# Attention and two feed-forward layers: seventh products into an output bank, larger batches in the shared bank, more groups in the seven-product form

## The chip, the cores and the metric

The kernel runs on one core of a Trainium2 chip. The metric is the device time of one execution in microseconds, the median of three runs.

## What is computed

`x` is an attention output over 6016 tokens of 256 channels, where the scores are channels against channels (256 x 256). Two feed-forward layers follow, with 2048 hidden features each:

```python
def _moe_ref(x, w_in, w_out):        # layer one
    h = x @ w_in
    r = np.maximum(h, 0.0)
    g = r * r
    return (g @ w_out).astype(np.float32)

def _moe2_ref(x, w_in, w_out):       # layer two
    h = x @ w_in
    g = np.maximum(0.01 * h, h)
    return (g @ w_out).astype(np.float32)
```

All data are fp32.

## The kernel before

**Tiling.** The tokens are cut into six pairs of halves, 512 tokens a half in five pairs and 448 in the fifth (`WIDTH`). The hidden features are cut into eight groups of 256 (`NG`), two blocks of 128 each. The layers run pair by pair, and in a pair group by group: 12 sweeps of eight groups, 96 units `n`. Layer one's first pair has the attention folded into its weights and a form of its own; the other 88 units are built by `unit`.

**Number form.** [...] Each fp32 operand is split into a high part (a cast by ScalarE) and a low part (a subtraction by VectorE, line 120), and a product is three matmuls (`mm3`): low by high, high by high, high by low.

**First products.** For one group the products of input and `w_in` form a 2 x 2 block product (two token halves, two feature blocks, two channel blocks). It is computed in seven block products, F1 to F7, in place of eight, after Strassen and Winograd. Two banks hold them, `ha` and `hb` (in plain pairs alternately `hc` and `he`). ScalarE copies a bank out between them (`C11`, `u`, `w`; line 1378), VectorE adds (`c22`, `c12`: `c<-w` and `c<-u`, line 570), and TensorE goes on in the same bank when the copy or sum is there. F6 is the seventh in order. The next group's F2 goes into a bank that ScalarE's copy `C11` has filled, and that copy waits for the sum `c12` of the group before.

**Second products.** A group's activations `g` times `w_out` add up in the output banks `y`: (half, channel block) = (0,0), (0,1), (1,0), (1,1), over all eight groups of a pair. A *plain* group needs eight products. A *shared* group (`form_of` is "S", listed in `GROUPS`) needs seven, P1 to P7 (`shared_item`, with the tables `FROM` and `TO`), after the same identity. For it VectorE forms four differences of activations (`sub`, line 1473), and ScalarE and VectorE make high and low parts of five operands: G0 and G1 (1024 columns), B22, T3 and T2 (512 columns). P2, P3 and P4 go into the output banks (0,1), (1,1) and (0,0); P5 into a bank F of its own; P1, P6 and P7 into one bank A in turn.

**Shared sums.** What stands in A is taken out by `take_shared` after every batch of two groups (`BATCH`): into P1, then U (P6), then V (P7). The first batch is copied by ScalarE, later ones are added by VectorE. Five shared groups make batches of two, two and one. At a pair's end `combine` (in the last pair `combine_last`) joins P1, U, V, F and the output banks in six additions of VectorE; in layer two the result is transposed and stored. Pairs with shared groups are called mixed: before, layer one's last two and all of layer two.

**What sets the order.** The kernel first plans: `build` lists tasks with an engine, a cost, a due time, what they depend on and which buffers they need (`Buf`; `link` makes the k-th user of a buffer wait for the user that had it before). `simulate` runs a list schedule with these costs (`PIPE` gives latencies), and `PE.choose` takes first products in order and fills between them with the second products that are ready. Several turns are made (`TURNS`); the plan with the earliest end for TensorE is written out. From there the order on each engine is fixed, and each engine executes in its order. All loads and stores are issued by SyncE, in order. Weights of shared groups are loaded in three parts: `wo` (512 KB), `ws` for P5 (128 KB) and `ws` for P6 and P7 (256 KB).

Of the kernel before, what the change touches and what calls it, by code (L numbers as in the profile page):

```python
# [26 lines left out]
def raw(ap):  # L27
    return ap.bitcast(F32)
# [3 lines left out]
def attn_moe_moe2(  # L32
# [22 lines left out]
    GROUPS = {(1, 4): (0,1,3,4,6), (1, 5): (0,1,3,4,6), **{(2, p): (0,1,3,4,6) for p in range(5)}, (2, 5): (0,1,3,4)}  # L55
# [61 lines left out]
    order.__enter__()  # L117
# [217 lines left out]
    with (  # L335
# [3 lines left out]
    ):  # L339
        acc = att.tile([P, 2, G, C], F32, name="acc")  # L340
# [313 lines left out]
    def shared(n, product, bank_key, first):  # L654
# [92 lines left out]
    def take_out(key, d):  # L747
# [73 lines left out]

    def simulate(pe):
        for i, x in enumerate(tasks):
            x.then, x.then_order = [], []
            if late_start and x.engine in ("DVE", "ACT"):
                x.due = late_start[i]
# [13 lines left out]
        while n:  # L840
# [109 lines left out]
    BATCH = 2  # L950
    FROM = {"P1": "G0", "P2": "G0", "P3": "B22", "P4": "G1", "P5": "G1", "P6": "T2", "P7": "T3"}
    TO = {"P1": "A", "P6": "A", "P7": "A", "P5": "F", "P2": ("y", 0, 1), "P3": ("y", 1, 1), "P4": ("y", 0, 0)}

    def batch_of(n):
        L, p, g = units[n]
        i = sorted(GROUPS[L, p]).index(g)
        return i // BATCH, i % BATCH

    def seeded(n):

        L, p, g = units[n]
        return L == 2 and not (p and g < 2 and WIDTH[p] > WIDTH[p - 1])
# [9 lines left out]
    def build(base):  # L972
# [141 lines left out]
        done = {}  # L1114
# [18 lines left out]
        def finish_plain(L, p):  # L1133
# [4 lines left out]
            for half in range(2):  # L1138
# [10 lines left out]
                b = T("DVE", 3.1 * s, due + 0.1, take_out, key, 1, deps=done[L, p, half, 1] + [a], uses=[o])  # L1149
# [165 lines left out]

        def load_wo(n):
# [50 lines left out]

# [430 lines left out]
```

## Time and profile before

| | us |
|---|---|
| median of three runs | 1013.92 |
| lowest and highest | 1013.14, 1014.22 |
| the profiled execution | 1014.96 |
| its span, first to last instruction | 1013.2 |
| TensorE busy | 1005.3 |
| VectorE busy | 878.5 |
| ScalarE busy | 793.5 |

The profile is of one execution. "Busy" is the time in which at least one instruction of the engine ran; instructions of VectorE and ScalarE overlap a little at their ends, so the distance between the starts of two queued ones is shorter than the duration of either. The granted clock of TensorE is 0.999 of its 2.4 GHz level over the span.

### The profile page before, as it was taken

How to read it: one execution, taken by the hardware profiler on the slowest of the kernel's cores; microseconds unless marked ns; L12 is line 12 of the kernel's file. 1: busy time of each engine (PE TensorE's matmuls, PEld its weight loads, DVE VectorE, ACT ScalarE, POOL GpSimd, SP SyncE). 2: the span in 40 equal slices, each digit the busy share in tenths (PEclk: the TensorE clock that was granted, in tenths of full speed). 3: DMA queues.
4: the chain of work that ended last, by engine and by line, in shares of the span. 5: the costliest groups of instructions: out<-in, count | busy, mean ns of one | idle time of the engine just before them, and what ended most of it. 6: DMA issues, size and time to landing. Idle time of an engine off the chain costs nothing.

```text
span 1013.2 us, 13102 instructions
## 1 busy us (share of the span) xinstructions
PE 1005.3 (99%) x4579; PEld 847.7 (84%) x4579; DVE 878.5 (87%) x1293; ACT 793.5 (78%) x1221; POOL 0.7 (0%) x6
## 2 busy tenths in 40 slices
PE   9999999999999999999999999999999999999998
PEld 7888887888888888998888888888888888898887
DVE  5999888999999999999999879979979978977975
ACT  6788778888879788988887777787777777776772
POOL 0000000000000000000000000000000000000000
PEclk9999999999999999999999999999999999999999
DMA  9795559769969969876566555755755665765733
GB/s 346 287 224 195 184 190 285 235 245 308 319 227 308 330 235 296 284 243 206 185 222 226 193 199 191 223 185 195 207 193 199 201 193 176 204 221 178 206 122 84
DMA packets 138882, 226.70 MB, mean 224 GB/s; under 512 B 52032, under 2 KB 76096, under 8 KB 136896
## 3 DMA queue, kind: packets, MB, share of 16 engines
q1 hardware_dynamic: 138096, 225.21, 67.5%
q8 instruction: 36, 0.59, 0.2%
q10 hardware_dynamic: 720, 0.66, 0.2%
q14 instruction: 30, 0.25, 0.1%
HBM read 181.01 MB, written 44.83 MB: 223 GB/s over the span
## 4 chain that ended last, share of the span: by engine, by line
PE 94%; DMA 3%; DVE 1%; SPq 1%; ACT 1%; issue 0%; DVEq 0%
PE y L561 36%; PE ha L561 20%; PE hb L561 15%; PE yA L561 8%; PE h L723 4%; PE hc L561 3%; PE yF L561 3%; PE sT L403 2%; PE he L561 2%; PE pw L269 1%; DMA qk<-in_k_dram 1%; DMA wi<-wi 1%; DMA qk<-in_q_dram 1%; DMA out_dram<-o 0%; SPq L240 0%
## 5 line engine op out<-in xcount | busy, mean ns | idle before, releaser
L561 PE MATMUL y<-g,wo 128*128 128x512 f32 (+1 forms) x1578 | 410.5, 386 | 0.0
L561 PEld LDWEIGHTS y<-g,wo 128*128 128x128 f32 x1578 | 296.1, 188 | 57.3
L120 DVE TENSOR_TENSOR g<-c,g 128x1024 fp32r<-128x1024 f32 (+1 forms) x192 | 229.1, 1199 | 42.5 <-ACT g L693 20.7
L561 PE MATMUL ha<-x,wi 128*128 128x512 f32 (+1 forms) x912 | 252.3, 385 | 1.1 <-ACT c L1378 1.1
L561 PEld LDWEIGHTS ha<-x,wi 128*128 128x128 f32 x912 | 171.0, 188 | 33.0 <-ACT c L1378 1.8
L561 PE MATMUL hb<-x,wi 128*128 128x512 f32 (+1 forms) x684 | 189.1, 385 | 0.0
L561 PEld LDWEIGHTS hb<-x,wi 128*128 128x128 f32 x684 | 128.2, 188 | 24.0 <-DVE c L570 0.2
L693 ACT CAST g<-c 128x1024 fp32r<-128x1024 f32 (+1 forms) x114 | 117.5, 1042 | 4.9 <-PE y L561 2.9
L1473 DVE TENSOR_TENSOR c<-c 128x512 f32<-128x512 f32 (+1 forms) x156 | 104.9, 673 | 4.6 <-ACT c L710 0.6
L708 ACT ACTIVATE c<-c 128x512 f32<-128x512 f32 (+1 forms) x160 | 97.7, 620 | 10.7 <-DVE c L568 8.4
L1451 ACT CAST g<-c 128x1024 fp32r<-128x1024 f32 (+1 forms) x78 | 79.8, 1023 | 9.1 <-DVE c L1473 3.9
L120 DVE TENSOR_TENSOR b<-c,b 128x512 fp32r<-128x512 f32 (+1 forms) x117 | 76.7, 669 | 5.3 <-ACT b L1466 5.1
L1378 ACT COPY w<-ha 128x512 f32<-128x512 f32 (+1 forms) x76 | 43.7, 575 | 45.0 <-PE ha L561 44.8
L1466 ACT CAST b<-c 128x512 fp32r<-128x512 f32 (+1 forms) x117 | 69.1, 607 | 8.3 <-PE y L561 3.1
L710 ACT ACTIVATE c<-c 128x512 f32<-128x512 f32 (+1 forms) x98 | 59.7, 620 | 7.6 <-DVE c L570 7.4
L561 PE MATMUL yA<-b,ws 128*128 128x512 f32 (+1 forms) x234 | 60.6, 383 | 0.0
L561 PEld LDWEIGHTS yA<-b,ws 128*128 128x128 f32 x234 | 43.9, 188 | 7.8
L1378 ACT COPY u<-ha 128x512 f32<-128x512 f32 (+1 forms) x76 | 43.7, 575 | 8.4 <-PE ha L561 4.8
L723 PE MATMUL h<-x,wi 128*128 128x512 f32 x192 | 47.9, 390 | 0.0
L120 DVE TENSOR_TENSOR x<-xr,x 128x1024 fp32r<-128x1024 f32 (+3 forms) x44 | 46.4, 1064 | 0.2 <-ACT x L1216 0.2
L570 DVE TENSOR_TENSOR c<-u,hb 128x512 f32<-128x512 f32 (+1 forms) x48 | 32.4, 674 | 15.6 <-PE hb L561 15.2
L1392 ACT ACTIVATE c<-ha 128x512 f32<-128x512 f32 (+1 forms) x48 | 28.2, 587 | 22.1 <-PE ha L561 21.7
(130 smaller groups left out, 1209.7 us busy)
## 6 DMA issues: line engine op xcount, KB each, us to landing
wi<-wi SPq DMA_DIRECT2D x80, 896.0 KB, 5.6
wo<-wo SPq DMA_DIRECT2D x86, 512.0 KB, 4.8
wi<-wi SPq DMA_DIRECT2D x24, 512.0 KB, 4.7
wst<-in_moe_w_in_dram SPq DMA_DIRECT2D x16, 512.0 KB, 5.6
wst<-in_moe_w_out_dram SPq DMA_DIRECT2D x16, 512.0 KB, 6.3
ws<-wo SPq DMA_DIRECT2D x29, 256.0 KB, 3.2
wi<-wis SPq DMA_DIRECT2D x8, 896.0 KB, 5.9
wo<-wos SPq DMA_DIRECT2D x13, 512.0 KB, 5.7
```

Of the source, the lines that this page charges most:

```text
L120: tt(lo, x, raw(hi), op=ALU.subtract)
L561: nc.tensor.matmul(ps, a[m], b[n], start=first and i == 0, stop=i == 2, skip_group_check=True)
L570: tt(to, a, b, op=ALU.add)
L693: nc.scalar.copy(g_t[n, half][:, 0, :, :w], c)
L708: nc.scalar.activation(c, c, AF.Square)
L710: nc.scalar.activation(c, c, AF.Prelu, alpha=0.01)
L723: nc.tensor.matmul(h_t[n, half, fb][:, :w], a[i], b[j], start=start, stop=stop, skip_group_check=True)
L1378: nc.scalar.copy(to, h(0))
L1392: nc.scalar.activation(to, h(0), AF.Prelu, alpha=0.01)
L1451: nc.scalar.copy(g_t[n, name][:, 0, :, :w], result(n, half, w))
L1466: nc.scalar.copy(b_t[n, name][:, 0, :w], c(half, fb))
L1473: tt(c(*to), c(*a), c(*b), op=ALU.subtract)
```

## The change

1. P7 no longer goes into A. It adds up in the output bank (1,0) over the whole pair (`TO`), beside nothing else until the shared groups are done. Then ScalarE copies the bank to V, once per pair, and the plain group's products go on in the same bank (`shot`). P7's sum so stands both in V and in the output bank (1,0).
2. A holds P1 and P6 only, in batches of three or four groups (`BATCHES`).
3. `combine` is rewritten: V becomes V + U, U becomes U + F, and the sum from bank (1,0) (`y22`) is made from U and bank (1,0) in a buffer of its own, before the sum from bank (1,1) (`y12`) is added into U.
4. The shared groups stand at the front of a pair: seven of eight in layer two (five in its last pair, four before), six in layer one's last two pairs.
5. The weights of P5, P6 and P7 are loaded as three transfers of 128 KB. T3 shares a buffer with B22; T2 waits in buffers until its batch ends.
6. In layer one a whole tile of 1024 columns is squared at once in place of two halves (`WHOLE`).
7. The planner has other latencies and costs (`PIPE`), may wait 0.6 for a task that is more urgent (`AWAIT`), makes 12 turns, and puts P5, P4 and P7 of the group before ahead of a group's own (`LATE_FIRST`). `NOISE`, `SEEDS` and `OUTS` leave things as they are. `ident` and `zeros` move to a pool that ends with the attention.

```diff
-    GROUPS = {(1, 4): (0,1,3,4,6), (1, 5): (0,1,3,4,6), **{(2, p): (0,1,3,4,6) for p in range(5)}, (2, 5): (0,1,3,4)}
+    GROUPS = {(1, 4): tuple(range(6)), (1, 5): tuple(range(6)), **{(2, p): tuple(range(7)) for p in range(5)}, (2, 5): tuple(range(5))}
...
-    PIPE = {"DVE": (0, 0.3), "ACT": (0, 0.3), "PE": (0, 0.3), "POOL": (0, 0.3)}
+    PIPE = {"DVE": (0.09, 0.45), "ACT": (0.1, 0.5), "PE": (0, 0.5), "POOL": (0, 0.6)}
...
-    BATCH = 2
-    TO = {"P1": "A", "P6": "A", "P7": "A", "P5": "F", "P2": ("y", 0, 1), "P3": ("y", 1, 1), "P4": ("y", 0, 0)}
+    TO = {"P1": "A", "P6": "A", "P7": ("y", 1, 0), "P5": "F", "P2": ("y", 0, 1), "P3": ("y", 1, 1), "P4": ("y", 0, 0)}
+    BATCHES = {4: (4,), 5: (3, 2), 6: (3, 3), 7: (4, 3)}
...
+            if (half, d) == (1, 0):
+                deps.append(shot.get((L, p)))
...
-            n11 = e11 if seed else nl(0, 1, e11, 20)
+            if L == 1 and WHOLE:
+                n11 = n21 = T("ACT", A2, t0 + 38, nonlinear, n, 0, w, "square", deps=[e11, e21], uses=[cb[0]])
+                n22 = n12 = T("ACT", A2, t0 + 44, nonlinear, n, 1, w, "square", deps=[e22, e12], uses=[cb[1]])
...
-                nc.scalar.copy(sum_t[L, p, which][:, :w], a())
+                nc.scalar.copy(sum_t[L, p, which][:, :w], a() if which != "V" else y_t[L, p, 1, 0][:, :w])
...
-            if b == 0:
+            if b == 0 or which == "V":
...
+                late = [f_done[-1], shared_item(n - 1, "P4")]
+                p7 = shared_item(n - 1, "P7")
+                p7_done.append(p7)
+                if ends:
+                    take_shared(L, p, "P1", b, list(in_batch))
+                    p6 = [shared_item(m, "P6") for m in range(n - size, n)]
+                    take_shared(L, p, "U", b, p6)
+                if g == len(gs):
+                    take_shared(L, p, "V", 0, [*p7_done, got["U"]])
+                    shot[L, p] = got["V"]
...
+            uv = T("DVE", D1, t0 + 40, lambda: add(S("V"), S("V"), S("U")), deps=[got["U"], got["V"]], uses=[B[L, p, "U"]])
+            fu = T("DVE", D1, t0 + 42, lambda: add(S("U"), S("U"), f()), deps=[uv, *f_done], uses=[B[L, p, "U"]])
             y11 = T("DVE", D1, t0 + 40, lambda: add(S("P1"), S("P1"), y(0, 1)), deps=[got["P1"], *Y(0, 1)], uses=[B[L, p, "P1"]])
+            y21 = T("DVE", D1, t0 + 45, lambda: add(S("V"), S("V"), y(0, 0)), deps=[uv, *Y(0, 0)], uses=[B[L, p, "V"]])
-            y12 = T("DVE", D1, t0 + 53, lambda: add(S("U"), S("U"), y(1, 1)), deps=[fu, *Y(1, 1)], uses=[B[L, p, "U"]])
-            y22 = T("DVE", D1, t0 + 56, lambda: add(S("V"), S("V"), y(1, 0)), deps=[fv, *Y(1, 0)], uses=[B[L, p, "V"]])
+            y22 = T("DVE", D1, t0 + 53, x_new, deps=[fu, *Y(1, 0)], alloc=B[L, p, "X"], uses=[B[L, p, "U"]])
+            y12 = T("DVE", D1, t0 + 56, lambda: add(S("U"), S("U"), y(1, 1)), deps=[y22, *Y(1, 1)], uses=[B[L, p, "U"]])
```

The order moves on every engine. Three places follow. In the rows, `ha<-x0` opens a group (F1), the next row of a bank with `x3` or `x2` goes on in it, and numbers behind names are tile numbers, which differ between the kernels.

The first place is TensorE in layer one's second pair, at the change from its second to its third group. Before:

```order
L561 MATMUL hc_1459<-x3_1317,wi_1275 128x512 x3
L561 MATMUL y_689<-g_1383,wo_1349 128x512 x3
L561 MATMUL he_1493<-x1_1235,wi_1275 128x512 x3
L561 MATMUL y_1540<-g_1478,wo_1351 128x512 x3
L561 MATMUL y_1547<-g_1478,wo_1351 128x512 x3
L561 MATMUL y_1540<-g_1478,wo_1351 128x512 x3
L561 MATMUL y_1547<-g_1478,wo_1351 128x512 x3
L561 MATMUL y_1571<-g_1498,wo_1351 128x512 x3
L561 MATMUL ha_1577<-x0_1159,wi_1469 128x512 x3
```

After:

```order
L562 MATMUL y_691<-g_1391,wo_1323 128x512 x3
L562 MATMUL hc_1460<-x3_1312,wi_1283 128x512 x3
L562 MATMUL y_1531<-g_1479,wo_1325 128x512 x3
L562 MATMUL he_1494<-x1_1200,wi_1283 128x512 x3
L562 MATMUL y_1544<-g_1479,wo_1325 128x512 x3
L562 MATMUL y_1531<-g_1479,wo_1325 128x512 x3
L562 MATMUL y_1544<-g_1479,wo_1325 128x512 x3
L562 MATMUL y_1572<-g_1502,wo_1325 128x512 x3
L562 MATMUL y_1576<-g_1502,wo_1325 128x512 x3
L562 MATMUL y_1572<-g_1502,wo_1325 128x512 x3
L562 MATMUL ha_1588<-x0_1163,wi_1472 128x512 x3
```

From the last `hc` product of the second group six second products stood ahead of the next F1, now seven; and the one of the first group that was among the six (`y_689`, now `y_691`) stands ahead of `hc`. So two more are done before the third group begins.

The second place is VectorE in layer two's second pair, from the end of its third group to that of its fourth. Before, the third group is plain:

```order
L120 TENSOR_TENSOR g_5990<-c_5849,g_5990 128x1024
L120 TENSOR_TENSOR b_5885<-c_5805,b_5885 128x512
L120 TENSOR_TENSOR b_5983<-c_5878,b_5983 128x512
L570 TENSOR_TENSOR acc_5406<-acc_5406,y_5431 128x512
L636 STREAM_TRANSPOSE o_6041<-acc_5406 128x16x32
L120 TENSOR_TENSOR g_6035<-c_5934,g_6035 128x1024
L120 TENSOR_TENSOR g_6043<-c_5964,g_6043 128x1024
L570 TENSOR_TENSOR c_6068<-w_6054,hb_6029 128x512
L636 STREAM_TRANSPOSE o_6041<-acc_5406 128x16x32
L120 TENSOR_TENSOR b_5966<-c_5878,b_5966 128x512
L120 TENSOR_TENSOR g_6074<-c_6018,g_6074 128x1024
L570 TENSOR_TENSOR c_6068<-u_6027,hb_6029 128x512
```

After, both are shared; `c<-c` are the differences, `b` and `g` low parts:

```order
L116 TENSOR_TENSOR g_6002<-c_5934,g_6002 128x1024
L1526 TENSOR_TENSOR c_5934<-c_5977,c_5934 128x512
L1526 TENSOR_TENSOR c_5977<-c_5977 128x512
L116 TENSOR_TENSOR b_6023<-c_5977,b_6023 128x512
L1526 TENSOR_TENSOR c_5977<-c_5977,c_5934 128x512
L1526 TENSOR_TENSOR c_5934<-c_5934,c_5977 128x512
L116 TENSOR_TENSOR b_6023<-c_5977,b_6023 128x512
L571 TENSOR_TENSOR c_6062<-w_6055,hb_6037 128x512
L116 TENSOR_TENSOR b_5883<-c_5885,b_5883 128x512
L637 STREAM_TRANSPOSE o_6075<-acc_5575 128x16x32
L116 TENSOR_TENSOR g_6067<-c_5934,g_6067 128x1024
L571 TENSOR_TENSOR c_6062<-u_6034,hb_6037 128x512
```

A low part of 1024 columns (`g_5991`) stands between the third group's `c<-u` and the first row after; a transpose, a low part and another low part stand there before. The four differences and the low parts of B22 and T3 (both `b_6023`) now stand where low parts of earlier groups, an addition and transposes stood. TensorE beside it, after, from the fourth group's F6 to the second F product of the next group:

```order
L562 MATMUL hb_6037<-x1_5145,wi_5814 128x512 x3
L562 MATMUL yA_5915<-g_6002,wo_5760 128x512 x3
L562 MATMUL ha_6086<-x0_5126,wi_5906 128x512 x3
L562 MATMUL y_5936<-g_6002,wo_5760 128x512 x3
L562 MATMUL y_5942<-b_6023,wo_5760 128x512 x3
L562 MATMUL yF_5958<-g_6067,ws_5993 128x512 x3
L562 MATMUL hb_6099<-x1_5145,wi_5906 128x512 x3
```

Five products stand between the two `hb` rows, with the first row six.

The third place is the change from layer one's last pair to layer two's first. VectorE before:

```order
L570 TENSOR_TENSOR acc_4710<-acc_4710,yA_5087 128x512
L570 TENSOR_TENSOR acc_4710<-acc_4710,yF_4635 128x512
L570 TENSOR_TENSOR c_5194<-u_5172,hb_5175 128x512
L570 TENSOR_TENSOR acc_4710<-acc_4710,y_4579 128x512
L570 TENSOR_TENSOR acc_5227<-acc_4710,y_4643 128x512
L120 TENSOR_TENSOR g_5196<-c_5063,g_5196 128x1024
L570 TENSOR_TENSOR acc_4710<-acc_4710,yF_4635 128x512
```

After:

```order
L571 TENSOR_TENSOR c_5165<-w_5157,hb_5141 128x512
L571 TENSOR_TENSOR acc_4781<-acc_4781,y_4548 128x512
L116 TENSOR_TENSOR b_5121<-c_5086,b_5121 128x512
L116 TENSOR_TENSOR g_5170<-c_5058,g_5170 128x1024
L571 TENSOR_TENSOR c_5165<-u_5138,hb_5141 128x512
L116 TENSOR_TENSOR b_5163<-c_5086,b_5163 128x512
L571 TENSOR_TENSOR acc_5206<-acc_4781,y_4561 128x512
L571 TENSOR_TENSOR acc_4781<-acc_4781,y_4521 128x512
```

Before, the sum from bank (1,1) (`y_4579`) stood right behind the group's `c<-u`, ahead of the one from bank (0,0) (`y_4643`), and the one from bank (1,0) came eleven rows further on. Now the sum from bank (1,1) (`y_4521`) is the last of the four, behind low parts and the one from bank (1,0) (`y_4561`). TensorE after:

```order
L562 MATMUL y_4561<-g_5071,wo_4822 128x512 x6
L562 MATMUL yA_5202<-g_5102,wo_4896 128x512 x3
L562 MATMUL hb_5200<-x1_4454,wi_5027 128x512 x3
L562 MATMUL ha_5186<-x3_4831,wi_5027 128x512 x3
L562 MATMUL y_5225<-g_5102,wo_4896 128x512 x3
L562 MATMUL hb_5232<-x2_4479,wi_5027 128x512 x3
L562 MATMUL ha_5186<-x2_4479,wi_5027 128x512 x3
L562 MATMUL y_5243<-b_5121,wo_4896 128x512 x3
```

Row one holds the last two products of the old pair's bank (1,0), the last row is P3 of the new pair, into the bank that `acc_4781<-acc_4781,y_4521` reads.

## Rows read from the trace of the kernel before

**Rows 1.** The page: busy us of each engine, share of the span, instructions.
```profile
PE 1005.3 (99%) x4579; PEld 847.7 (84%) x4579; DVE 878.5 (87%) x1293; ACT 793.5 (78%) x1221; POOL 0.7 (0%) x6
```
**Rows 2.** TensorE's waits: for whom, us in total, times, longest.
```profile
PE sT L403 <- DMA qk<-in_k_dram: 1.4, 2, 1.2
PE ha L561 <- ACT c L1378: 1.1, 1, 1.1
...
```
**Rows 3.** Pairs of tokens: stretch, length, busy us (instructions) by engine, clock, DMA.
```profile
143.70:222.60 78.90, 77.82 (x343) 64.07 (x342) 69.92 (x119) 63.96 (x98) 0.00 (x0) 1.00 0.81 252
222.60:304.20 81.60, 81.60 (x361) 67.57 (x360) 76.02 (x127) 67.43 (x101) 0.00 (x0) 1.00 0.83 283
...
456.80:532.10 75.30, 75.30 (x338) 62.98 (x337) 69.79 (x96) 64.56 (x104) 0.00 (x0) 1.00 0.61 203
...
612.50:690.70 78.20, 78.20 (x346) 64.75 (x345) 67.77 (x90) 60.86 (x95) 0.00 (x0) 1.00 0.61 200
...
919.40:1013.20 93.80, 89.92 (x424) 76.09 (x423) 68.04 (x96) 58.39 (x90) 0.00 (x0) 0.99 0.48 147
```
**Rows 4.** TensorE in order of time: start, us, line, operation, count.
```profile
502.75 0.84 PE L561 MATMUL hb<-x,wi 128*128 128x512 f32 x3
503.43 0.84 PE L561 MATMUL yA<-b,ws 128*128 128x512 f32 x3
...
504.79 0.84 PE L561 MATMUL hb<-x,wi 128*128 128x512 f32 x3
```
**Rows 5.** The same, second products of 448 tokens.
```profile
935.04 0.77 PE L561 MATMUL y<-g,wo 128*128 128x448 f32 x3
935.65 0.77 PE L561 MATMUL yA<-b,ws 128*128 128x448 f32 x3
```
**Rows 6.** The chain that ended last, in order of time, before 166.66 us.
```profile
151.80 8.95 DMA wi<-wi
...
166.13 0.48 ACT c L1378
...
166.66 0.96 PE ha L561 x3
```
**Rows 7.** VectorE in order of time, queued instructions.
```profile
592.37 0.68 DVE L570 TENSOR_TENSOR c<-u,hb 128x512 f32<-128x512 f32 x1
592.96 0.69 DVE L120 TENSOR_TENSOR b<-c,b 128x512 fp32r<-128x512 f32 x1
593.57 1.22 DVE L120 TENSOR_TENSOR g<-c,g 128x1024 fp32r<-128x1024 f32 x1
594.70 0.69 DVE L120 TENSOR_TENSOR b<-c,b 128x512 fp32r<-128x512 f32 x1
...
606.06 2.14 DVE L1473 TENSOR_TENSOR c<-c 128x512 f32<-128x512 f32 x3
```
**Rows 8.** ScalarE's casts of 512 columns, a group: count, busy us, mean ns, idle before.
```profile
L1466 ACT CAST b<-c 128x512 fp32r<-128x512 f32 (+1 forms) x117 | 69.1, 607 | 8.3 <-PE y L561 3.1 <-DVE c L1473 1.7 <-PE yA L561 0.8
```
**Rows 9.** DMA issues: operation, count, KB each, median us to landing.
```profile
ws<-wo SPq DMA_DIRECT2D x29, 256.0 KB, 3.2
...
ws<-wo SPq DMA_DIRECT2D x29, 128.0 KB, 3.7
...
ws<-wos SPq DMA_DIRECT2D x10, 256.0 KB, 4.3
```
**Rows 10.** All engines' waits, VectorE's longest.
```profile
DVE g L120 <- ACT g L693: 20.7, 31, 2.6
DVE g L120 <- ACT g L1451: 20.4, 25, 3.2
```
**Rows 11.** SyncE's waits before it issues, the longest.
```profile
SPq L1281 <- PE hb L561: 166.3, 59, 8.2
```
**Rows 12.** VectorE's groups from 560 to 860 us, shapes apart: mean ns.
```profile
L120 DVE TENSOR_TENSOR g<-c,g 128x1024 fp32r<-128x1024 f32 x61 | 74.0, 1223 | 20.7 <-ACT g L693 10.4 <-ACT g L1451 9.8
L1473 DVE TENSOR_TENSOR c<-c 128x512 f32<-128x512 f32 x74 | 51.0, 690 | 2.3 <-ACT c L710 0.6
```

More of the change, by code (lines that the diff above doesn't have):

```diff
@@ L1 @@
+import random
 from contextlib import ExitStack
@@ L663, in shared @@
         else:
-            a = both(late_w[n, "S23"], {"P6": 0, "P7": 1}[product])
+            a = both(late_w[n, "S2" if product == "P6" else "S3"], 0)
         x = {"P1": lambda: both(g_t[n, "G0"], 0, sl), "P2": lambda: both(g_t[n, "G0"], 1, sl),
@@ L856, in simulate @@
                 x = min((x for x in open_[e] if x.ready <= t), key=lambda x: x.due)
+                if AWAIT and late_start and e in ("ACT", "DVE"):
+                    y = min((y for y in open_[e] if y.ready <= t + AWAIT), key=lambda x: x.due)
+                    if y.due < x.due - 2:
+                        x, t = y, max(t, y.ready)
                 open_[e].remove(x)
@@ new lines, in load_wo, with load_s2 @@
+            _, i, size = batch_of(n)
+            def load_s2():
+                if i % 2 == 0:
+                    t = cpool.tile([P, 2, 2, P], F32R, tag="ce", name="ws")
+                    late_w[n, "S2"] = t[:, :, :1]
+                    late_w[n, "next"] = t[:, :, 1:]
+                else:
+                    late_w[n, "S2"] = late_w[n - 1, "next"]
+                nc.sync.dma_start(raw(late_w[n, "S2"]), sums_d[:, :, 6:7])
+            wo_ready[L, p, g] = T("SP", "wo", base[n] + 13, load, alloc=b, lat=LOAD, deps=[dep])
@@ L1399, in c12, with take, c11_seeded, c21 @@
                 add(result(n, 1, w, 1), s_t[n, "u"][:, :w], h(1), L == 1)
+            def take(half, fb, bank_):
+                to = result(n, half, w, fb)
+                if L == 1:
+                    nc.scalar.activation(to, h(bank_), AF.Relu)
+                else:
+                    nc.scalar.activation(to, h(bank_), AF.Prelu, alpha=0.01)
+            def c11_seeded():
+                new_result(n, 0)
+                take(0, 1, 1)
+            def c21():
+                take(0, 0, 0)
             A1, A2, D1, D2 = 2.7 * s, 4.6 * s, 3 * s, 5.4 * s
@@ L1566, in mixed_items @@
             gs = sorted(GROUPS[L, p])
-            prev = n - 1 if g - 1 in gs else None
-            ends = prev is not None and (batch_of(prev)[1] == BATCH - 1 or g - 1 == gs[-1])
+            assert gs == list(range(len(gs)))
+            late, p6, ends = [], [], False
+            if g - 1 in gs:
+                b, i, size = batch_of(n - 1)
+                ends = i == size - 1
+                f_done.append(shared_item(n - 1, "P5", first=g == 1))
+                late = [f_done[-1], shared_item(n - 1, "P4")]
[3 more added lines that the diff above has]
+                    take_shared(L, p, "P1", b, list(in_batch))
+                    in_batch.clear()
+                    p6 = [shared_item(m, "P6") for m in range(n - size, n)]
[3 more added lines that the diff above has]
+                    shot[L, p] = got["V"]
+                    p7_done.clear()
+                for y in (*late, p7, *p6):
+                    y.n = n
             if form_of(n) == "S":
-                p1 = shared_item(n, "P1", first=batch_of(n)[1] == 0) if not ends else None
+                p1 = shared_item(n, "P1", first=batch_of(n)[1] == 0)
+                in_batch.append(p1)
                 own = [shared_item(n, "P2"), shared_item(n, "P3")]
-                early = [p1, *own] if p1 else own
-                own = []
+                own = own if ends else [p1, *own]
+                if LATE_FIRST:
+                    items.extend([*late, *([p7] if late else []), *own, *p6, *([p1] if ends else [])])
+                else:
+                    items.extend([*own, *late, *([p7] if late else []), *p6, *([p1] if ends else [])])
             else:
```

174 lines of the change are left out of this document (82 added, 92 removed).

## The prediction

> **What bounds the kernel now.** I read the busy line of the page first: TensorE is busy 1005.3 of 1013.2 us, VectorE 878.5, ScalarE 793.5 [rows 1]. The list of TensorE's waits is almost empty: nothing in it is longer than 1.4 us, and one entry alone, 1.1 us, lies behind the start [rows 2]. Cut at the starts of the token pairs, every pair but the second (the 1.1 us) and the last (the end) shows TensorE busy for its whole length [rows 3]. So the time is the number of TensorE's columns plus about 8 us at the two ends and in that one wait. A second product that is left out shortens the end directly, as long as nobody makes TensorE wait. The question is what the other engines have left: VectorE is busy 67.77 of 78.20 us in a pair of layer two, and 76.02 of 81.60 us in the densest pair, a plain one of layer one; TensorE waited in neither [rows 3].
>
> **Products removed.** A plain group has eight second products, a shared one seven. Before, 10 + 25 + 4 = 39 groups are shared, after it 12 + 35 + 5 = 52, so 13 products of three matmuls go; the lists of TensorE's instructions differ by the same 39. Three of the 13 lie in the pairs of 448 tokens. Products of 512 start 0.68 us apart [rows 4], of 448 columns 0.61 us [rows 5]: 10 x 0.68 + 3 x 0.61 = **8.63 us off**, all on the path. The additions P7 makes in the output bank cost TensorE what they did in the shared one.
>
> **The one wait in the middle.** At 166.66 us TensorE has stood 1.1 us for a copy of ScalarE; the chain leads back to a load of 8.95 us [rows 6]. In the new order two second products more stand ahead of that place, 1.36 us of work that was later. If the copy comes when it did, the wait is gone (1.1 us off); if the load slips, nothing is won. I take **0.8 us off**, nearer the first, since 1.36 covers 1.1.
>
> **VectorE's work.** Queued instructions of 512 columns start 0.59 to 0.61 us apart, one of 1024 gives way after 1.13 us [rows 7]; where each needs the one before, three take 2.14 us, some 0.72 each [rows 7]. A shared group costs nine of 512, two of 1024 and two such dependences: 9 x 0.60 + 2 x 1.14 + 0.24 = 7.92 us; a plain one 2 x 0.60 + 2 x 1.14 = 3.48. Two groups more per pair of layer two add 8.9 us. Six additions out of the shared bank become two, since batches of two, two, one become four, three, and the seventh products need none: 4 x 0.60 = 2.4 us off. The six additions at a pair's end stay six. So a pair goes from 67.77 to 74.3 us. From below: 7 x 7.92 + 3.48, the next pair's inputs 6.5, eight additions 4.8 (and 0.4 where they depend), four transposes 2.5, together 73.1 (the same sum for the kernel before gives 66.6, against 67.77 measured). TensorE's pair becomes 78.20 - 2 x 0.68 = 76.84 us. VectorE is left 2.5 to 3.7 us instead of 10.4: **95 to 97% full**. In layer one each mixed pair gains one shared group: 69.79 + 4.4 - 2.4 = 71.8 of 75.30 - 0.68 = 74.6 us, 96%. The conversions added in front of them, low parts of 1024 columns for one more set of weight sums and for two more weights stored in blocks, with small additions, come to some 5 us by the same distances, spread over pairs that hold 93% already [rows 3]. I cost this work at nothing where it lies beside TensorE; its cover is these 2.5 to 3.7 us, and beyond them each us is a us of the end, per pair.
>
> **Does it fit group by group?** A mean does not make TensorE wait, a place does. I went down the new order of VectorE from one group's last sum (`c<-u`) to the next, at the distances above, and beside it TensorE from one seventh first product to the next. Before, only two groups, at the start of the second pair, ask more of VectorE than of TensorE. Now about 15 do: half of them by under 0.3 us, the fourth group of three layer-two pairs with 9.7 against 8.8 us (its rows stand with the change), the worst, the last group of layer one's third pair, by 1.9. What covers this is the stretch from the seventh first product to the next group's second one, in which VectorE adds and ScalarE copies. In the kernel before it is 2.04 us at 502.75 us, without a wait [rows 4]; in the fourth group it is now six products, 4.08 us, so 2 us are to spare for 0.9. In the worst place it is 3.40: 1.36 to spare for 1.9, a wait of **0.5 us**.
>
> **The pair's end.** Before, the sum from bank (1,1) needed the one with F alone; now it comes behind the one from bank (1,0) as well, since both read one buffer. P3 of the next pair's first group writes the bank it reads. TensorE has six products, 4.08 us, between the last plain product and that P3. VectorE still has a low part of 512, one of 1024, an addition and another low part ahead of the two sums: 0.6 + 1.14 + 0.6 + 0.6 + 1.3, and 0.2 to be noticed: 4.4 us if none has begun, 1.5 if all have. That is 0 to 0.4 us at each of seven ends, up to 2.8. Both low parts ahead can run before, so I take 0.15 each: **1.0 us on**.
>
> **ScalarE and the loads.** ScalarE gets three casts of 0.61 us per new group (117 of them stand in the trace [rows 8]), 24 us, eight copies, and 80 whole squares for 160 halves, which cannot add: at most 823 us of some 1005, 82%. The copy of the seventh products' sum waits for VectorE, with ScalarE's next copies behind it; it comes once a pair, with four products of cover in the last pair's order. Off the path, 0. Of late weights, what came as 128 and 256 KB comes as three of 128 KB; a half-size load lands no sooner (3.7 us against 3.2 [rows 9]). The Trainium skill, "DMA: Bandwidth & Descriptors", "Rules for kernel authors", asks for the contrary, few transfers of 1 MiB; these rows agree that halving saves nothing, and by it the sum here would change only if a load came late. Three buffers serve fifth and seventh products; from the product that frees one to the product that needs its next content lie 16 products, 10.9 us, against 3.7. I take 0.
>
> **The sum.** -8.63 - 0.8 + 0.5 + 1.0 = -7.9 us. The profiled execution took 1014.96 us for a span of 1013.2, 1.04 above the median of the runs; from 1014.96 it gives 1007.0, from the median 1013.92 the predicted **1006.0 us**.
>
> **Rivals.** (1) *VectorE cannot fill its queue.* It idles because it waits, in order, for casts: 20.7 and 20.4 us in all for two kinds of them [rows 10]. If it needs as much idle time as the densest pair shows, 5.6 us, a pair of layer two lasts 74.3 + 5.6 = 79.9 us, 1.7 more than before, a mixed one of layer one about as much; over seven pairs 12 us: **1026, slower**. It decides at 78.2 - 74.3 = 3.9 us of idle time per pair; below 2.5 it costs nothing. For it: no stretch of this kernel shows VectorE above 93% of a pair. Against: as its load rose from 87% to 93% its idle time fell from 10.4 to 5.6 us and TensorE still never waited, so the idle time looks like what is left over. (2) *Half way*: it needs 3.1 to 3.6 us per pair and seven pairs give back 4 to 7 us of the 9.4 won: 1008.5 to 1011.9. (3) *Equal*: 3.6 to 4.2 us, 1011.9 to 1016. (4) *A late weight load.* SyncE issues in order and has waited up to 8.2 us for a buffer of first weights [rows 11]; 8.2 + 4.3 [rows 9] = 12.5 us against 10.9: 1.6 us late, if at every pair 8 x 1.6: 1019. Against: the trace has no TensorE wait for a weight load. (5) *Each instruction of VectorE takes its whole duration*, 0.69 and 1.22 us [rows 12]: the pair sums to 79.6 us, 1.4 over the old length; seven pairs: 1024. Against: the same sum makes the old pair 72.7, and 67.77 was measured; and the starts in [rows 7]. The Trainium skill, "VectorE: DVE Perf Modes", "The DRAIN you can't avoid", says that after each instruction the next one does not start until the pipe is empty, which would be this case (it excepts instructions that are not held). The trace agrees with the exception only: 0.60 us between starts at 0.69 long.
>
> **How the numbers follow.** Forecast, 1003.6 to 1008.5: 0.66. Half way: 0.13. Equal: 0.06. Slower: rival 1 0.09, rival 4 0.04, rival 5 0.02. The range is 1003.6 (no stall at all, 1.1 won, and 0.6 for the scatter of the median) to 1011.5, which holds the first two. A measurement tells about 0.2%, 2 us, from no change: faster 0.79, same 0.06, slower 0.15.
>
> **What would show it.** Right: 39 matmuls fewer, TensorE busy about 996.7 us and its list of waits under 4 us in all; layer-two pairs of 76.8 to 77.2 us with VectorE at 73 to 74.5; the wait near 166 us gone. Wrong: pairs of 78 us or more, with TensorE waiting on `c` or `hb` copies behind VectorE (rivals 1 to 3, 5), or on `ws` loads (4); a wait before the third second product of a pair means the pair's end was undersized.

## The result, and the profile after

| | before | after |
|---|---|---|
| median of five runs each, us | 1013.19 | 1005.54 |
| lowest and highest | 1012.38, 1014.22 | 1004.12, 1006.27 |
| ratio, 95% interval | | 0.992 (0.9906 to 0.9933) |
| the profiled execution, us | 1014.96 | 1005.90 |
| its span | 1013.2 | 1004.1 |
| matmuls | 4579 | 4540 |

The changed kernel is 0.8% faster; 1006.0 was predicted. The busy line of its page, to hold against [rows 1]:

```profile
PE 998.2 (99%) x4540; PEld 840.8 (84%) x4540; DVE 920.8 (92%) x1371; ACT 803.7 (80%) x1181; POOL 0.7 (0%) x6
```

TensorE has 39 matmuls fewer and is 7.1 us less busy, VectorE has 78 instructions more and is 42 us busier. Nobody makes TensorE wait for long: its whole list of waits (for whom, us in total, times, longest), to hold against [rows 2], is

```profile
PE warm L369 <- DVE small L363: 1.1, 1, 1.1
PE eT L497 <- ACT e L491: 0.3, 1, 0.3
PE sT L404 <- DMA qk<-in_k_dram: 0.2, 1, 0.2
PE ha L562 <- ACT u L1421: 0.2, 1, 0.2
```

The first three lie in the attention. By token pairs, in the columns of [rows 3], layer one's last pair, then layer two's first four and its last:

```profile
456.70:534.00 77.30, 77.30 (x346) 64.70 (x346) 72.45 (x99) 64.02 (x91) 0.00 (x0) 1.00 0.63 204
534.00:609.80 75.80, 75.78 (x334) 62.43 (x333) 70.71 (x95) 64.17 (x101) 0.00 (x0) 1.00 0.64 222
609.80:688.80 79.00, 79.00 (x350) 65.29 (x349) 74.97 (x101) 65.02 (x102) 0.00 (x0) 1.00 0.67 216
688.80:766.60 77.80, 77.80 (x344) 64.05 (x343) 73.97 (x101) 64.25 (x102) 0.00 (x0) 1.00 0.64 210
766.60:842.80 76.20, 76.20 (x338) 63.05 (x337) 72.33 (x100) 62.68 (x99) 0.00 (x0) 1.00 0.67 215
...
911.00:1004.10 93.10, 89.20 (x421) 75.49 (x419) 75.21 (x106) 60.09 (x95) 0.00 (x0) 0.99 0.50 153
```

A cut lies at a pair's first product, and second products of the pair before fall on either side of it (334 to 350 matmuls between cuts), so the four pairs of layer two are read together: 77.2 us each, of which VectorE is busy 73.0 and idle 4.2. The same four stretches before were 78.8 us long. What VectorE had waited in order for casts of ScalarE [rows 10], 20.7 and 20.4 us, is now 7.0 and 3.1:

```profile
DVE g L116 <- ACT g L694: 7.0, 18, 1.4
DVE g L116 <- ACT g L1501: 3.1, 7, 0.8
```

So most of its idle time was indeed what was left over, and the new work went into it. At the place of [rows 6] there is no wait any more. TensorE in order of time:

```profile
160.13 4.24 PE L562 MATMUL y<-g,wo 128*128 128x512 f32 x18
164.22 0.84 PE L562 MATMUL ha<-x,wi 128*128 128x512 f32 x3
...
166.25 0.84 PE L562 MATMUL ha<-x,wi 128*128 128x512 f32 x3
```

At the place called the worst, the beginning of layer one's fourth pair, it does stand (a bracket at a row's end says how long the engine had stood, and for whose result):

```profile
303.62 1.52 PE L562 MATMUL y<-g,wo 128*128 128x512 f32 x6
305.13 0.96 PE L562 MATMUL ha<-x,wi 128*128 128x512 f32 x3
...
306.62 0.86 PE L562 MATMUL hb<-x,wi 128*128 128x512 f32 x3
307.66 0.96 PE L562 MATMUL ha<-x,wi 128*128 128x512 f32 x3 [0.17 <-ACT u L1421]
```

Six matmuls should give way after 1.36 us and do so after 1.51; three after 0.68, and the last `ha` comes 1.04 behind `hb`. That is 0.15 and 0.36 beyond the matmuls' own distances, 0.5 us in all. Both `ha` rows wait for ScalarE's copies (`c`, `u`). ScalarE, then VectorE, there:

```profile
303.55 1.05 ACT L205 CAST wis<-wr 128x1024 fp32r<-128x1024 f32 x1 [1.03 <-DMA wo<-wis]
304.50 0.58 ACT L1421 COPY c<-ha 128x512 f32<-128x512 f32 x1
```
```profile
305.11 0.69 DVE L569 CUSTOM_DVE_ANT_0 c<-c,hb 128x512 f32<-128x512 f32 x1 [0.98 <-ACT c L1421]
```

A cast of ScalarE had stood 1.03 us for a transfer out of its buffer (converted weights, `wo<-wis`), the copies were queued behind it, and VectorE itself stood 0.98 us for the first of them. In e4_vec3 below, whose order is the same up to layer two, that transfer landed after 8.8 us in place of 9.3 and was not waited for:

```profile
302.90 1.06 ACT L205 CAST wis<-wr 128x1024 fp32r<-128x1024 f32 x1 [0.53 <-DVE c L569]
```

The first of the two delays is gone there, and 0.14 us of the second is left. "Excess" below means this: what the distances between TensorE's starts hold beyond 0.227 us for a matmul of 512 columns and 0.203 for one of 448, counted behind the attention and where it is above 0.03 us.

### The profile page after: what moved, and what is told of

The parts are those of the page before. It is cut to its first block, busy times and chain, and to the rows that moved or that the text cites. A ratio compares the mean times of both kernels' runs of the same rounds, so it can differ in the third digit from the quotient of the medians.

```text
span 1004.1 us, 13173 instructions
## 1 busy us (share of the span) xinstructions
PE 998.2 (99%) x4540; PEld 840.8 (84%) x4540; DVE 920.8 (92%) x1371; ACT 803.7 (80%) x1181; POOL 0.7 (0%) x6
## 4 chain that ended last, share of the span: by engine, by line
PE 95%; DMA 3%; ACT 1%; DVE 1%; SPq 0%; issue 0%; ACTq 0%; DVEq 0%
PE y L562 36%; PE ha L562 20%; PE hb L562 15%; PE yA L562 7%; PE h L724 4%; PE yF L562 3%; PE hc L562 3%; PE sT L404 3%; PE he L562 2%; PE pw L265 1%; DMA qk<-in_k_dram 1%; DMA wo<-wis 1%; DMA qk<-in_q_dram 1%; DMA out_dram<-o 0%; ACT c L701 0%; ACT wis L205 0%
## 5 line engine op out<-in xcount | busy, mean ns | idle before, releaser
L562 PE MATMUL y<-g,wo 128*128 128x512 f32 (+1 forms) x1344 | 350.5, 387 | 0.0
L562 PEld LDWEIGHTS y<-g,wo 128*128 128x128 f32 x1344 | 252.2, 188 | 49.1
L1526 DVE TENSOR_TENSOR c<-c 128x512 f32<-128x512 f32 (+1 forms) x208 | 139.9, 673 | 7.4
L116 DVE TENSOR_TENSOR b<-c,b 128x512 fp32r<-128x512 f32 (+1 forms) x156 | 102.9, 668 | 1.7 <-ACT b L1519 1.6
L701 ACT ACTIVATE c<-c 128x1024 f32<-128x1024 f32 (+1 forms) x96 | 100.2, 1044 | 1.5
L711 ACT ACTIVATE c<-c 128x512 f32<-128x512 f32 (+1 forms) x98 | 60.7, 621 | 7.7 <-DVE c L571 7.5
L562 PE MATMUL y<-b,ws 128*128 128x512 f32 (+1 forms) x156 | 43.0, 384 | 0.0
L562 PE MATMUL yA<-g,wo 128*128 128x512 f32 (+1 forms) x156 | 43.0, 384 | 0.0
L562 PE MATMUL y<-b,wo 128*128 128x512 f32 (+1 forms) x156 | 43.0, 384 | 0.0
L562 PE MATMUL yF<-g,ws 128*128 128x512 f32 (+1 forms) x156 | 43.0, 383 | 0.0
```

Of the source, the lines that this page charges most:

```text
L116: tt(lo, x, raw(hi), op=ALU.subtract)
L562: nc.tensor.matmul(ps, a[m], b[n], start=first and i == 0, stop=i == 2, skip_group_check=True)
L701: nc.scalar.activation(c, c, AF.Square)
L711: nc.scalar.activation(c, c, AF.Prelu, alpha=0.01)
L1526: tt(c(*to), c(*a), c(*b), op=ALU.subtract)
```

## The experiments

All ratios are to the kernel before on the same chip. That kernel took 1014.77 us on the chip of e4, e3, e7 and e2 and 1013.19 to 1013.24 on the others, so differences between kernels are taken from the ratios below, as shares of 1013.2 us. "Span" is that of the profiled execution.

| kernel | us | ratio, 95% interval | span |
|---|---|---|---|
| the changed kernel | 1005.54 | 0.992 (0.9906 to 0.9933) | 1004.1 |
| e1_five | 1012.46 | 0.9994 (0.9984 to 1.0003) | 1010.8 |
| e5_before_costs | 1013.42 | 1.0002 (0.9993 to 1.0012) | 1011.8 |
| e4_vec3 | 1009.89 | 0.9954 (0.9939 to 0.9968) | 1007.6 |
| e3_vec7 | 1019.84 | 1.005 (1.0035 to 1.0065) | 1018.8 |
| e7_vec14 | 1050.21 | 1.0354 (1.0337 to 1.0371) | 1045.1 |
| e8_batch2 | 1012.48 | 0.9996 (0.9986 to 1.0005) | 1009.0 |
| e2_seven_l1 | 1013.67 | 0.9988 (0.9978 to 0.9998) | 1011.9 |
| e6_old_plan | 1022.96 | 1.0092 (1.0077 to 1.0107) | 1021.3 |
| f1_old_pipe | 1018.01 | 1.0043 (1.0029 to 1.0057) | 1018.8 |
| f2_half_squares | 1006.49 | 0.9938 (0.9918 to 0.9958) | 1005.2 |
| f3_own_first | 1020.13 | 1.0062 (1.0047 to 1.0078) | 1016.3 |
| f4_no_await | 1008.35 | 0.995 (0.9935 to 0.9964) | 1007.6 |

### Is it the products?

**e1_five**: the changed kernel, with five shared groups in every mixed pair.

```diff
-    GROUPS = {(1, 4): tuple(range(6)), (1, 5): tuple(range(6)), **{(2, p): tuple(range(7)) for p in range(5)}, (2, 5): tuple(range(5))}
+    GROUPS = {(1, 4): tuple(range(5)), (1, 5): tuple(range(5)), **{(2, p): tuple(range(5)) for p in range(5)}, (2, 5): tuple(range(5))}
```

> The changed kernel with five shared groups in every mixed pair (40 in place of 52), all else as in the change: batches, P7 in the output bank, new plan. Theory A (TensorE's products set the time): 12 products come back, 9 x 0.68 + 3 x 0.61 = 7.95 us, so 1012 to 1013.5 us, with VectorE near 80% of a layer-two pair. Rival B (the gain comes from fewer additions and the new order, and the products are hidden): 1006 to 1008.

**e5_before_costs**: the kernel before, with the changed kernel's latencies in the planner and its 12 turns.

```diff
-    PIPE = {"DVE": (0, 0.3), "ACT": (0, 0.3), "PE": (0, 0.3), "POOL": (0, 0.3)}
+    PIPE = {"DVE": (0.09, 0.45), "ACT": (0.1, 0.5), "PE": (0, 0.5), "POOL": (0, 0.6)}
...
-    TURNS = 8
+    TURNS = 12
```

> The kernel before with the planner's new latencies and 12 turns alone; groups and products as before. Theory A: TensorE was full, so nothing but the one wait of 1.1 us can go: 1012 to 1014. Rival B (the new plan is the gain): 1008 or less.

With the 12 products back (9 of 512 columns, 3 of 448: 7.95 us by [rows 4, 5]) the gain is gone: 0.9994 against 0.992 is 7.5 us. All else, P7 in the output bank, batches, loads, the planner's settings, is still there and wins nothing by itself. Both runs came out as theory A said. In e5 the 1.1-us wait near 166 us is gone too, and its span is 1.4 us shorter than that of [rows 3], but the medians show no gain, to within 0.1%: a term of 0.8 us is at the edge of what medians tell.

### How much more could VectorE take?

**e4_vec3**, **e3_vec7**, **e7_vec14**: in layer two, behind the low part of T2, the same subtraction is done over again; once for three of the groups, once for each shared group, or twice. The planner doesn't know of them, so TensorE's order is word for word the changed kernel's. They are 18, 40 and 80 instructions of 0.60 us more. The diff of e3:

```diff
                 low(b[:, 1, :w], c(half, fb), b[:, 0, :w])
+                for _ in range(1 if L == 2 and name == "T2" else 0):
+                    low(b[:, 1, :w], c(half, fb), b[:, 0, :w])
```

(e4 adds `and g in (0, 2, 4)` to the condition, e7 has 2 in place of 1.)

> The changed kernel, unplanned: the low part of T2 is made twice in three of the seven shared groups of each layer-two pair (18 extra instructions of 512 columns). TensorE's order is word for word that of the change. 3 x 0.6 to 0.72 = 1.8 to 2.2 us more for VectorE per pair against 3.8 idle. Theory A: 1005 to 1007.5. Rival C (1:1): 18 x 0.6 = 11 us, 1016.

> As the run with three, but in all shared groups of layer two (40 extra instructions): 4.2 to 5.0 us per pair against 3.8 idle. Theory A: over the cover by 0.4 to 1.2 us in five pairs, so 1007 to 1013. Rival C (1:1): 40 x 0.6 = 24 us, 1029. Rival D (VectorE has far more room than its busy time shows): 1005 to 1006.

> As before, each T2 low part of layer two three times (80 extra instructions): 8.4 to 10 us per pair against 3.8 idle. Theory A: 4.6 to 6.2 us over in each of some five and a half pairs, 1028 to 1040. Rival C (1:1): 80 x 0.6 to 0.72 = 48 to 58 us, 1053 to 1063. Rival D: under 1015.

| layer two's first four pairs, mean us | length | VectorE busy | idle | TensorE's waits for `c` (L571), whole run |
|---|---|---|---|---|
| e1_five | 78.2 | 65.3 | 12.9 | none |
| changed kernel | 77.2 | 73.0 | 4.2 | none |
| e4_vec3 | 78.3 | 74.7 | 3.5 | 1.5, 4 times |
| e3_vec7 | 79.8 | 76.8 | 3.0 | 5.3, 11 times |
| e7_vec14 | 84.7 | 81.4 | 3.3 | 23.0, 20 times |

The rows of the third pair in e3 and e7, and TensorE's longest entry in e7's list:

```profile
694.50:774.60 80.10, 79.24 (x343) 63.53 (x342) 77.47 (x107) 64.05 (x102) 0.00 (x0) 1.00 0.63 204
```
```profile
702.40:786.80 84.40, 79.86 (x343) 63.36 (x342) 81.55 (x113) 64.01 (x102) 0.00 (x0) 1.00 0.60 193
```
```profile
PE hb L562 <- DVE c L571: 23.0, 20, 2.5
```

No theory's range held in these three: e4 lies between A and C, e3 between A and C, e7 (1050.21) between A and C as well, and D is far off. So it is no step. Of 1.7 us more work in a pair 1.05 come back as length, of 3.8 us 2.6, of 8.4 us 7.5. By the ratios an added instruction of 0.60 us costs 0.19 us at first, 0.44 between 18 and 40, 0.77 beyond. Layer two alone lasts 470.1 us in the changed kernel's profile, then 475.7, 484.6 and 513.0: that is 0.31, 0.40 and 0.71 each. VectorE's mean idle time does not fall below 3.0 us: 96% is full here, and the changed kernel has less than one us per pair to spare.

The trace shows where the next us goes. A group hands TensorE two sums that free the bank `hb`: `c<-w` and, later, `c<-u`. VectorE, then TensorE, in a fourth group of the changed kernel:

```profile
664.44 0.69 DVE L116 TENSOR_TENSOR b<-c,b 128x512 fp32r<-128x512 f32 x1
665.11 0.69 DVE L571 TENSOR_TENSOR c<-w,hb 128x512 f32<-128x512 f32 x1
665.71 0.71 DVE L637 STREAM_TRANSPOSE o<-acc 128x512 f32<-128x512 f32 x1
```
```profile
665.65 0.84 PE L562 MATMUL ha<-x,wi 128*128 128x512 f32 x3
666.33 0.84 PE L562 MATMUL hb<-x,wi 128*128 128x512 f32 x3
```

The sum ends at 665.80, 0.53 us before the product that needs its bank. The same place in e3, with one more `b` ahead:

```profile
669.02 1.41 DVE L116 TENSOR_TENSOR b<-c,b 128x512 fp32r<-128x512 f32 x2
670.35 0.68 DVE L571 TENSOR_TENSOR c<-w,hb 128x512 f32<-128x512 f32 x1
```
```profile
669.93 0.84 PE L562 MATMUL ha<-x,wi 128*128 128x512 f32 x3
671.09 0.96 PE L562 MATMUL hb<-x,wi 128*128 128x512 f32 x3 [0.31 <-DVE c L571]
```

Now the product follows 0.06 us after the sum, and TensorE has waited. Over all 48 groups of layer two, the median from the end of `c<-w` to the next product in `hb` is 0.59 us before, 0.53 after, 0.44 in e4, 0.23 in e3, 0.08 in e7; it is under 0.3 us in 3, 6, 17, 27 and 27 groups. For `c<-u` it is 1.83, 1.50, 1.38, 1.30 and 1.17. The thin cover is at `c<-w`, and it was thin before. Of TensorE's excess in layer two, some two thirds stand right behind that sum: 3.5 of 5.4 us in e4, 9.7 of 14.3 in e3, 28.7 of 42.6 in e7.

There is a second thin place, ScalarE's copy into `hb`, which opens the next group: its median cover is 0.54 us before, 0.53 after and still 0.47 in e7, and 0.6, 3.3 and 9.1 us of the excess stand behind it. In e7 it is the next entry of TensorE's list:

```profile
PE hb L562 <- ACT hb L1421: 6.7, 8, 1.2
```

This copy in turn waits for VectorE's sum ahead of it (14.1 us in all in e7, 6.7 in the changed kernel), so that sum counts too, by way of ScalarE.

### Batches of two, and a seventh group in layer one

**e8_batch2**: the shared bank is emptied every two groups again; VectorE has 934.1 us.

```diff
-    BATCHES = {4: (4,), 5: (3, 2), 6: (3, 3), 7: (4, 3)}
+    BATCHES = {4: (2, 2), 5: (2, 2, 1), 6: (2, 2, 2), 7: (2, 2, 2, 1)}
```

> The changed kernel with batches of two in the shared bank (seven groups: two, two, two, one): four more additions of VectorE per layer-two pair, 2.4 us, planned with the rest. Theory A (idle time of 3.8 us covers them): 1005 to 1008, VectorE 97 to 98% of a pair. Rival C (VectorE is already at its limit, every us more is a us of the end): seven pairs x 2.4 = 17 us, 1022.

The 26 additions, 13.3 us of VectorE, cost 7.7 us of the time together with the new plan that they bring, so without larger batches the change would have won nothing. The profiled execution's span is 4.9 us longer than the changed kernel's; 4.9 us of excess lie in layer two's last two pairs, and no earlier one shows over 0.9 us. Neither theory's range held.

**e2_seven_l1**: seven shared groups in layer one's two mixed pairs as well.

```diff
-    GROUPS = {(1, 4): tuple(range(6)), (1, 5): tuple(range(6)), **{(2, p): tuple(range(7)) for p in range(5)}, (2, 5): tuple(range(5))}
+    GROUPS = {(1, 4): tuple(range(7)), (1, 5): tuple(range(7)), **{(2, p): tuple(range(7)) for p in range(5)}, (2, 5): tuple(range(5))}
```

> The changed kernel with seven shared groups in layer one's two mixed pairs too (54 in place of 52): 0.61 + 0.68 = 1.3 us fewer products, and 4.0 + 4.4 us more for VectorE there, which then asks 99 to 100% of the first of the two pairs. Theory A: gain and waits nearly even out, 1004 to 1007. Rival C: 1012.

Two products fewer, and 6.9 us more: near rival C, and theory A is out. 5.9 us of excess are in layer one's fifth pair, most of it behind one wait of 3.6 us for VectorE's `c`. So six was the limit there for this planner.

### Is the planner's part free?

**e6_old_plan**: the changed kernel with all settings of the planner, and the half squares, as before.

```diff
-    PIPE = {"DVE": (0.09, 0.45), "ACT": (0.1, 0.5), "PE": (0, 0.5), "POOL": (0, 0.6)}
+    PIPE = {"DVE": (0, 0.3), "ACT": (0, 0.3), "PE": (0, 0.3), "POOL": (0, 0.3)}
...
-    LATE_FIRST = True
+    LATE_FIRST = False
...
-    AWAIT = 0.6
+    AWAIT = 0
...
-    WHOLE = True
+    WHOLE = False
...
-    TURNS = 12
+    TURNS = 8
```

> The changed kernel with the old planner settings (old latencies, no waiting for urgent tasks, 8 turns, own products first) and half squares in layer one; 52 shared groups. Theory A: the products stay away and VectorE's 3.8 us of idle time per layer-two pair cover a worse order: 1005 to 1008.5. Rival B (the order is what makes 95% possible): 1010 or more, with TensorE waiting in many places.

The same 13 products are gone, and it is slower than the kernel before: rival B, with eight entries behind the attention in TensorE's list of waits, one of them over 1 us. 8.0 of 17.6 us of excess lie in layer one's fifth pair, 6.7 of them in one wait of TensorE and the slow matmuls behind it. ScalarE's copy, VectorE and TensorE there:

```profile
418.51 0.52 ACT L1421 COPY w<-ha 128x448 f32<-128x448 f32 x1
```
```profile
420.47 0.62 DVE L116 TENSOR_TENSOR b<-c,b 128x448 fp32r<-128x448 f32 x1
421.00 1.94 DVE L1526 TENSOR_TENSOR c<-c 128x448 f32<-128x448 f32 x3
422.86 0.69 DVE L178 SCALAR_TENSOR_TENSOR cm<-cm,ce 128x512 f32<-128x512 f32 x1
423.46 0.62 DVE L116 TENSOR_TENSOR b<-c,b 128x448 fp32r<-128x448 f32 x1
423.99 2.09 DVE L116 TENSOR_TENSOR g<-c,g 128x896 fp32r<-128x896 f32 x2
426.00 0.62 DVE L116 TENSOR_TENSOR b<-c,b 128x448 fp32r<-128x448 f32 x1
426.53 0.62 DVE L569 CUSTOM_DVE_ANT_0 c<-w,hb 128x448 f32<-128x448 f32 x1
```
```profile
427.20 1.49 PE L562 MATMUL hb<-x,wi 128*128 128x448 f32 x3 [3.99 <-DVE c L569]
```

`w` was there at 419.03; the sum that needs it starts 7.5 us later, since VectorE works without a gap through what stands ahead. Before the runs that follow I summed the orders as the prediction does: from one `c<-u` to the next this group asks 14.5 us of VectorE against 9.8 of TensorE. That is theory W of the next four.

**f1_old_pipe**, **f2_half_squares**, **f3_own_first**, **f4_no_await**: one of these settings alone goes back, each by the line that e6's diff shows for it (PIPE, WHOLE, LATE_FIRST, AWAIT). TURNS alone was not tried.

> The changed kernel with the planner's old latencies (PIPE) alone. By the order's sums, which count VectorE's rows from one c<-u to the next at the distances of [rows 7], and TensorE's rows from one seventh first product to the next, the worst groups now ask 13.3 us of VectorE against 9.0 of TensorE and 11.9 against 9.2 in layer one's fifth pair, 15.3 against 12.9 at the end of its third, 14.0 against 11.6 and 16.2 against 14.3 at the ends of layer two's first two. Theory W (what costs is the excess of the worst groups beyond the 1.4 to 2 us that the cover gives, not a pair's mean): 1 + 4 to 7 + 1 + 1 + 0.5 us lost, so 1012 to 1017, most of it in layer one's fifth pair. Rival M (only a pair's mean share of VectorE counts, and it is 90 to 95% here as in the changed kernel but in that one pair): 1005 to 1007.

> The changed kernel with layer one's squares in two halves again (WHOLE) alone. The worst group by the order's sums is the last of layer one's third pair, 12.5 us of VectorE against 10.2 of TensorE; the others ask at most 1.2 us more than TensorE. Theory W (excess of the worst group beyond 1.4 to 2 us): 0.3 to 1 us lost, 1005 to 1007. Rival H (half squares were what cost the time in the kernel with all old settings, since ScalarE and the rows that wait for it are then late in layer one): 1010 or more, lost in layer one's mixed pairs.

> The changed kernel without the rule that P5, P4 and P7 of the group before stand ahead of a group's own (LATE_FIRST) alone. The order is word for word the changed kernel's up to layer one's fourth pair. In its fifth one group asks 15.3 us of VectorE against 10.4 of TensorE; the next worst, in layer two, ask 11.0 against 8.2 and 10.4 against 8.8. Theory W (excess of the worst group beyond 1.4 to 2 us): 3 to 6 us in that one group and 1 to 2 in layer two, so 1009 to 1014, with the wait for a sum of VectorE in layer one's fifth pair. Rival M (only a pair's mean share counts, 95% there and in the changed kernel's layer two alike): 1005 to 1007.

> The changed kernel without the planner's waiting for a more urgent task (AWAIT 0) alone. No group asks over 1.7 us more of VectorE than of TensorE (10.5 against 8.8 in one of layer two). Theory W (excess of the worst group beyond 1.4 to 2 us): 0 to 1 us lost, 1004.5 to 1006.5. Rival A (each of the settings is needed): 1009 or more.

Above the changed kernel, by the ratios: f2 1.8, f4 3.0, f1 12.5, f3 14.4 us. W tells the two cheap ones from the two dear ones. M falls by f1 and f3, H by f2; A comes near in f4 (1008.4 for 1009), but f2's setting is worth one or two us at most. W's sizes are too low for f3 and a little for f4 and f1, and it does not find every place: in f1 it finds the fifth pair of layer one with 5.4 us of excess (1.3 of them stand behind a load of `ws`), but 3.9 of its 16.4 us follow from a wait in order, not from a sum of work. ScalarE, VectorE, then TensorE, in layer one's fourth pair:

```profile
332.93 1.05 ACT L205 CAST wis<-wr 128x1024 fp32r<-128x1024 f32 x1 [3.12 <-DMA wos<-wis]
```
```profile
330.36 0.68 DVE L758 COPY o<-y 128x512 f32<-128x512 f32 x1
334.02 1.23 DVE L116 TENSOR_TENSOR wis<-wr,wis 128x1024 fp32r<-128x1024 f32 x1 [2.97 <-ACT wis L205]
335.16 0.68 DVE L569 CUSTOM_DVE_ANT_0 c<-w,hb 128x512 f32<-128x512 f32 x1
```
```profile
335.89 1.55 PE L562 MATMUL hb<-x,wi 128*128 128x512 f32 x3 [1.96 <-DVE c L569]
```

ScalarE's cast of converted weights stands 3.12 us for a transfer out of the buffer, VectorE's low part of the same weights 2.97 us for the cast, the sum for `hb` is queued behind it, and TensorE waits. In f3, 3.9 us of excess are in layer one's fifth pair, where W looks for them; but only a wait of 1.0 us there is for the sum that W names, and two of 1.0 each are for operands of P5 (`yF`). 9.0 us are in layer two, in all its pairs, and the list of TensorE's waits has several causes:

```profile
PE hb L562 <- ACT hb L1421: 1.7, 1, 1.7
PE yF L562 <- DVE g L116: 1.4, 2, 1.0
PE hb L562 <- DVE c L571: 1.2, 1, 1.2
...
PE y L562 <- DMA ws<-wo: 1.1, 2, 0.6
```

Operands of P5 and loads of `ws` now come late too. Which of them would be left if `c` were in time was not tried and stays open.

## Why the prediction was right, and where it was not

**Products: right.** 8.63 us were set down; 39 matmuls are gone, the span is 9.1 us shorter, and e1 gives back 7.5 us for products of 7.95.

**The wait near 166 us: right**, at the upper end: no wait is left there, 1.1 us off where 0.8 was taken. Counted from the pair's first product, `ha` is due 1.4 us later than before, as the two products say, and ScalarE's copy is done 0.3 us sooner. e5 shows that the planner's latencies and 12 turns alone remove it.

**The worst group: right in place and size, by luck.** 0.5 us was set down for the end of layer one's third pair, as VectorE's surplus of work, and 0.5 measured at its border. But there TensorE stands for ScalarE's copies behind a cast that waited 1.03 us for a transfer, and VectorE had time to stand 0.98 us; where the transfer was in time (e4), 0.14 us was left. So the step that turned VectorE's 1.9 us of surplus into a wait of 0.5 failed. Three smaller ones that weren't in the sum (0.11 at 397.6, 0.18 at 561.0 and 0.09 us at 762.7) make 0.4; the first and the last also stand behind casts of ScalarE that waited for transfers (0.54 and 1.18 us), the one at 561.0 is VectorE's `c<-w`.

**The pairs' ends: too dear.** 1.0 us was set down for seven ends; the list of waits has none there. No run shows the 0.2 us in that term for a sum to be noticed; in e3 the product starts 0.06 us after the sum that it waited for. Unforeseen, the start is 0.6 us shorter: a wait for an attention load of 1.4 us [rows 2] is 0.2 in this execution, for no reason that the runs show. -8.63 - 1.1 + 0.5 + 0.4 - 0.6 is -9.4, against -9.1 measured; the rest is products a few hundredths of a us longer.

**ScalarE and loads: right in the main.** ScalarE is busy 803.7 us, under the 823 set down, and no load of `ws` makes TensorE wait (120 loads of 128 KB land in 3.4 us, median). But the transfers that ScalarE's casts wait for were not among the loads that the prediction looked at, and some 0.7 us of TensorE's time stand behind them, as just said.

**VectorE's work: right.** 73.0 us per pair against 73.1 to 74.3; rival 5, with 79.6, is out, and queued starts are still 0.60 us apart at 0.69 long (665.11 and 665.71 above). By the Trainium skill, "VectorE: DVE Perf Modes", "The DRAIN you can't avoid", the next one would not start before the pipe is empty; these rows go on agreeing with its exception only.

**VectorE's cover: mis-sized.** The prediction let VectorE's work cost nothing within a cover of 2.5 to 3.7 us per pair, and one for one beyond. e4 has 3.5 us of idle time left and loses 3.4 us by the ratio, and no mean gets below 3.0. The step that failed is the choice of the stretch: I took the cover from the seventh product to the next group's second one, 2 us and more, and read it as the group's; the one that ends first is `c<-w`, with 0.5 us. The number came out because VectorE's work in a pair came to 73.0 us, the lower of the two sums. That is partly luck: at 74.3, the other sum, it would have been near e4's 74.7, whose pairs are 1.05 us longer, and e4's 1009.89 us lies in the range of rival 2, which was given 0.13. The loss begins within one us of VectorE per pair, where I had put the change well inside.

**The planner's settings, priced at nothing: wrong.** The planner's settings were costed only through the resulting order's sums. e6 says that without them, and with half squares, the change is 17 us slower and loses; f1 and f3 that two of them carry this, the latencies and the order of the group before. The sums that I made did see it, in part: in e6 the group with the largest surplus is where TensorE stands longest, in f3 it is one place of many, and in f1 a wait for a transfer, which no sum of work holds, costs 3.9 us.

## What to carry to other kernels

When an engine off the critical path is filled up, ask not for its mean share but for the shortest handover that it owes the bounding engine: the end of its result to the start of the instruction that needs it, over all groups. If the median there is one instruction long, the next instruction is already paid for in part. And a change that fills an in-order engine to 95% is worth what the order makes of it: predict the two together, and test the change with the old order. When a wait comes out where and as long as predicted, look at who ended it before calling the reason right.

## What I had not expected of the hardware

A long wait of TensorE can cost more than itself. In e6, from the wait on (stretch, length, busy us by engine, then the granted clock):

```profile
422.80:427.30 4.50, 0.51 (x4) 0.13 (x2) 4.50 (x8) 3.94 (x8) 0.00 (x0) 0.83 0.42 139
427.30:432.80 5.50, 5.50 (x15) 4.89 (x16) 3.30 (x7) 2.04 (x4) 0.00 (x0) 0.52 0.63 238
432.80:440.00 7.20, 7.20 (x36) 6.54 (x35) 6.51 (x12) 5.42 (x10) 0.00 (x0) 1.00 0.59 194
```

After the 4 us in which it stood, TensorE was granted 0.52 for 5.5 us, near its 1.2 GHz level, and by the distances of its matmuls that cost another 2.6 us. The same is in f1 behind the 1.96-us wait (0.52 for 3.5 us, 1.7 us lost) and in e2 behind 3.6 us (0.66 over 4.4 us). It does not follow every such wait: e7 has one of 2.5 us, and its clock stays at 1.00 in every pair.
